# RWKV attention with a Sinkhorn-gated MoE on one core: the bonus term of the first six tiles, taken from the diagonal of the masked scores

## The chip, the cores and the metric

The kernel runs on one core of a Trainium2 chip. Its time is device microseconds (us) of one execution, and the time before is the median of three runs: 1522.19 us (1521.31 to 1522.67). One more execution was taken with the hardware profiler; every duration below is from that one. Its five instruction streams are PE (TensorE, matmuls and transposes), DVE (VectorE), ACT (ScalarE), POOL (GpSimd) and SP, which here only issues DMAs. Each works through its own instructions in a fixed order, and waits for the others by semaphores.

## The reference

Two parts follow each other. The first is a linear attention with a decaying state for each of 4 batches and 8 heads, 768 tokens and a head dimension of 48; the second is a mixture of 8 experts over the 3072 x 384 rows that come out, whose gate is balanced by eight Sinkhorn rounds.

```python
for t in range(S):
    kt, vt, rt = (k[:, :, t], v[:, :, t], r[:, :, t])
    cur = np.einsum('bhd,bhe->bhde', u[None] * kt, vt)
    y[:, :, t] = np.einsum('bhd,bhde->bhe', rt, state + cur)
    state = w[None, :, :, None] * state + np.einsum('bhd,bhe->bhde', kt, vt)
...
for e in range(E):
    h = np.maximum(x @ w1[e], 0.0)
    ye = h @ w2[e]
    out += P[:, e:e + 1] * ye
```

The term with `u` is the bonus: token t sees its own value with the weight sum over d of r·u·k, one number for each token and head. All other tokens that t sees come through the state.

## The kernel before

**Tiles and stages.** The 3072 tokens are 24 tiles of 128 (6 tiles for a batch, `NCHB`). One loop, `for i in range(NTT + 3)` at line 852, runs the attention of all tiles as a software pipeline, and puts the matmuls of expert 0 (`g1_unit`, `g2_half`, handed out by `work`) between the tiles' steps, from iteration 4 on. After it come fourteen half experts, which are matmuls nearly back to back. Iteration i of the loop writes, in this order:

- `prep(i+2)`: r and k of tile i+2 are multiplied by tables of powers of w (`rtab` on POOL into `rp`, `ktab` on DVE into `kp`).
- `scale_x(i-2)`, `stage_e(i-2)`: the finished rows of tile i-2 are scaled and split in two float16 parts (`xsc`: the high part on ACT, the low part on DVE), then transposed by a DMA. For tile 2 PE does that (`turn_x`).
- `bonus_dot(i+1)`: POOL computes r·k and then r·k·u (`rk`).
- `stage_b(i+1)`: PE transposes `rp` and `kp`, ACT copies the results out of PSUM (`rT`, `kT`).
- loads of r and k of tile i+4.
- `bonus(i)`: DVE sums `rk` over d (`dg`), POOL multiplies v by it and adds a tile of zeros or channels done apart (`xadd`, in `hbx`).
- `stage_c(i)`: PE makes the scores (`pA`), DVE writes those below the diagonal over a tile of zeros (`at`, by `copy_predicated` under a mask). Since the mask never touches the rest, the two tiles `at_[0]` and `at_[1]` are filled with zeros once.
- `state_part`, `scores_part` of tile i-1 (`py`: state and scores times v), `state_product(i)` (`pu`), then DVE's `sum_x(i-1)` (`x` = `py` + bonus), `state_sum(i)` (`S`; POOL scales it), and `bound_x(i-1)` (`xm`, `xs`: the row's scale).
- at the places "loads", "early", "masked", "middle" and "end" the steps of `hooks`: the split of expert 0's weights into float16 pairs, by `magnitude` (ACT), `column_sums` (PE, `pcs`), `scale` (DVE), `high` (ACT), `low` (DVE).

**What sets the order.** It is the order written out in the program: the wrapper `InOrder` keeps each engine's instructions as they come. SP's DMA queue is in program order as well. PSUM has four banks for the attention (`ps3`), taken in turn by `prT`, `pkT`, the two `pA` and the two `py`; so a transpose of the next tile waits until the scores that held its bank have been read.

**The opening.** `spin(n)` issues n matmuls on zeros (`pz`) which compute nothing that is used. Ahead of the loop the tables are built: w is clamped (`wsafe`), its powers are scanned, inverted and transposed (`pt_tab`, copied by ACT to `rtab` and `ktab`). In the same stretch `hbx` (9216 columns) is zeroed by three engines, and a flag is computed on DVE which says whether any w lies out of range. Every engine loads the flag and branches past `scan_channels`, a slow path which these inputs do not take.

Of the kernel before, what the change touches and what calls it, by code (L numbers as in the profile page):

```python
# [33 lines left out]
def rwkv_sinkhorn_moe(  # L34
# [364 lines left out]
    fill(at_[0].rearrange("p h c -> p (h c)"))  # L399
# [4 lines left out]
    wlim = part(hb3, F32, 2496, (H, D))[:1]  # L404
    flag = ac.tile([1, 1], F32, name="flag")
# [5 lines left out]
    def scan_channels(scratch):  # L411

        BH = B * H
        yd = scratch.tile([B, S, DM], F32, name="yd")
        rows = [part(hbx, F32, i * BH * D, (BH, D))[:D] for i in range(4)]
        kb, rb, stt, kv = rows
        wn, wbad, wz = (part(hbx, F32, 4 * BH * D + i * H * D, (H * D,))[:D] for i in range(3))
        vt, yv = (part(hbx, F32, 5 * BH * D + i * BH, (BH,))[:D] for i in range(2))
        G.dma_start(wn, w.rearrange("(o h) d -> o (h d)", o=1).broadcast_to([D, H * D]))
        V.tensor_scalar(wbad, wn, W_MAX, W_MIN, op0=ALU.min, op1=ALU.max)  # L420
        V.tensor_tensor(wbad, wn, wbad, op=ALU.not_equal)
        V.memset(wz, 0.0)
        V.copy_predicated(wz, wbad.bitcast(I32), wn)
        V.memset(stt, 0.0)

        def of_b(x_):
            return x_.rearrange("p (b h) d -> p b (h d)", b=B)

        def for_b(x_):
            return x_.unsqueeze(1).broadcast_to([D, B, H * D])  # L430

        with tc.For_i(0, S, 1) as t:
            for dst, src in ((kb, k), (rb, r)):
                G.dma_start(
                    dst,
                    src.rearrange("b h s d -> s (b h) d")[bass.ds(t, 1)].broadcast_to([D, BH, D]),
                )
            G.dma_start(vt, v.rearrange("b h s d -> s d (b h)")[bass.ds(t, 1)].rearrange("o d a -> (o d) a"))
            V.tensor_tensor(rb, rb, stt, op=ALU.mult)
            V.tensor_reduce(yv, rb, axis=AX.X, op=ALU.add)  # L440
            for b in range(B):
                G.dma_start(
                    yd[b].rearrange("s (h d) -> s d h", d=D)[bass.ds(t, 1)].rearrange("o d h -> (o d) h"),
                    yv[:, b * H : (b + 1) * H],
                )
            V.tensor_tensor(of_b(kb), of_b(kb), for_b(wbad), op=ALU.mult)
            V.tensor_tensor(kv, kb, vt.unsqueeze(2).broadcast_to([D, BH, D]), op=ALU.mult)
            V.tensor_tensor(of_b(stt), of_b(stt), for_b(wz), op=ALU.mult)
            V.tensor_tensor(stt, stt, kv, op=ALU.add)
        yt = yd.rearrange("b s d -> (b s) d").rearrange("(t p) d -> p t d", p=P)  # L450
        for t in range(NTT):
            G.dma_start(xadd(t), yt[:, t, :])

    bad = nc.values_load(flag.bitcast(I32), min_val=0, max_val=0x3F800000)
    with tc.If(bad > 0):
        with tc.tile_pool(name="scratch", bufs=1, space=bass.MemoryType.DRAM) as scratch:
            scan_channels(scratch)

    load_part(2, "v", v)
    load_part(3, "v", v)  # L460
# [329 lines left out]
    def work(n, ready=True, hold=False):  # L790
        if not ready:
            spin(3)
            return
# [588 lines left out]
```

## Time and profile before

| what | before |
|---|---|
| median of three runs | 1522.19 us |
| the profiled execution | 1522.51 us, of which the span from the first to the last instruction is 1521.0 us |
| granted TensorE clock, mean | 0.999 |
| instructions | 29000 |
| zero matmuls (`pz`) | 52, the last at 36.1 us |

The rest of the profile is shown in the prediction, beside what is read from it. Nearly all lines of the trace carry line 30, that of the wrapper, so instructions are told apart by the names of what they write and read. A timeline row gives start, duration, engine, line, operation, output, inputs, shape and number; what follows in brackets is the idle time of that engine ahead of the row and what ended it. "SPq" and "ACTq" are DMA issues. A row of the view of stretches gives start and end, length, busy time and number for PE, PEld (weight loads), DVE, ACT and POOL, then the granted TensorE clock, the DMA share and GB/s.

### The profile page before, as it was taken

What the parts mean: (1) busy time and instruction counts of PE and PEld (TensorE: products, weight loads), DVE (VectorE), ACT (ScalarE), POOL (GpSimd) and SP (SyncE); (2) the same over time, 40 slices, a digit from 0 to 9 for tenths busy, and PEclk for the clock granted to TensorE, in tenths of its full rate; (3) what the DMA queues carried; (4) which work ended last, traced back from release to release, by engine and by line L of the source; (5) the groups of instructions that cost most, each with busy time, mean ns of one, the idle gap of its engine ahead of it and who ended that gap; (6) DMA issues with size and microseconds to landing.
All of it is one profiled execution on the core that took longest, in us unless ns stands there. A gap on an engine that the chain in (4) does not pass through costs nothing.

```text
span 1521.0 us, 29000 instructions
## 1 busy us (share of the span) xinstructions
PE 1502.5 (99%) x11729; PEld 848.4 (56%) x11729; DVE 1015.7 (67%) x1692; ACT 672.8 (44%) x1203; POOL 588.0 (39%) x685
## 2 busy tenths in 40 slices
PE   8899999999999999999999999999999999999999
PEld 5677765555555555555555555555555555555555
DVE  8898869586566666666676666666566666566464
ACT  5444435344354544545454444444354444445320
POOL 8779966010214234242524234242424233242200
PEclk9999999999999999999999999999999999999999
DMA  9756523211344675666656675655554554555434
GB/s 176 155 113 125 106 60 103 87 37 58 103 84 73 92 130 86 118 89 122 95 77 124 92 130 83 120 63 96 61 84 68 61 98 57 100 57 98 58 94 130
DMA packets 186441, 143.10 MB, mean 94 GB/s; under 512 B 108737, under 2 KB 180162, under 8 KB 186306
## 3 DMA queue, kind: packets, MB, share of 16 engines
q0 software_dynamic: 44928, 61.36, 32.8%
q1 hardware_dynamic: 141168, 79.87, 20.3%
q8 instruction: 92, 1.51, 0.4%
q14 instruction: 43, 0.35, 0.1%
q10 hardware_dynamic: 210, 0.00, 0.0%
HBM read 55.39 MB, written 80.23 MB: 89 GB/s over the span
## 4 chain that ended last, share of the span: by engine, by line
PE 93%; DVE 3%; POOL 1%; issue 1%; ACT 0%; DMA 0%; SPq 0%; POOLq 0%; DVEq 0%; ACTq 0%
PE po L30 49%; PE bZ L30 12%; PE bY L30 12%; PE ph L30 5%; PE bA L30 5%; PE bB L30 5%; PE bC L30 2%; PE py L30 2%; PE pA L30 1%; POOL rk L30 1%; DVE at L30 0%; PE pkT L30 0%; PE prT L30 0%; DVE xsc L30 0%; PE px L30 0%
## 5 line engine op out<-in xcount | busy, mean ns | idle before, releaser
L30 PE MATMUL po<-ws,hbx 128*128 128x384 f16 x3360 | 736.8, 326 | 0.0
L30 POOL DMA_DIRECT2D accd<-stg x288 | 250.5, 870 | 694.4 <-ACT stg L30 679.5
L30 PEld LDWEIGHTS <-hbx 128*128 128x128 f16 x3504 | 333.4, 98 | 292.1
L30 PEld LDWEIGHTS <-ws 128*128 128x128 f16 x3096 | 301.6, 98 | 248.5 <-issue 4.7
L30 ACT ACTIVATE hbx<-tb 128x512 f16<-128x512 f32 x224 | 141.0, 630 | 453.0 <-DVE tb L30 453.0
L30 PE MATMUL po<-ws,hb 128*128 128x384 f16 x1248 | 322.8, 326 | 0.0
L30 DVE TENSOR_TENSOR tb<-bY,tb 128x512 f32<-128x512 f32 x168 | 116.2, 692 | 176.3 <-PE bY L30 176.1
L30 ACT ACTIVATE stg<-po,pe 128x384 f32<-128x384 f32 x312 | 179.1, 574 | 122.1 <-PE po L30 99.1
L30 PE MATMUL bZ<-xv,ws 128*128 128x512 f16 x840 | 227.0, 379 | 0.8 <-DVE tb L30 0.8
L30 PE MATMUL bY<-xv,ws 128*128 128x512 f16 x840 | 227.0, 379 | 0.0
L30 DVE TENSOR_TENSOR tb<-bZ,tb 128x512 f32<-128x512 f32 x168 | 115.5, 687 | 135.8 <-PE bZ L30 135.8
L30 PEld LDWEIGHTS <-hb 128*128 128x128 f16 x1248 | 121.5, 98 | 93.0
L30 POOL TENSOR_TENSOR ucb<-rawb 128x256 f32<-128x256 f32 x84 | 75.8, 952 | 118.8 <-DMA rawb<-in_moe_w_dram 118.8
L30 DVE TENSOR_TENSOR tb<-bB,tb 128x512 f32<-128x512 f32 x112 | 77.4, 691 | 49.3 <-PE bB L30 47.4
L30 PE MATMUL ph<-hbx,ws 128*128 128x384 f16 x576 | 104.1, 326 | 3.0 <-issue 1.8
L30 DVE SCALAR_TENSOR_TENSOR hb<-tb,hbx 128x512 f16<-128x512 f32 x112 | 77.2, 689 | 24.6 <-ACT hbx L30 19.5
L30 PE MATMUL bA<-xv,ws 128*128 128x512 f16 x336 | 90.8, 379 | 0.0
L30 PE MATMUL bB<-xv,ws 128*128 128x512 f16 x336 | 90.8, 379 | 0.0
L30 DVE SCALAR_TENSOR_TENSOR hbx<-tb,hbx 128x512 f16<-128x512 f32 x112 | 78.8, 704 | 14.7 <-ACT hbx L30 10.4
L30 ACT COPY tb<-bZ 128x512 f32<-128x512 f32 x56 | 32.8, 586 | 65.4 <-PE bZ L30 65.4
L30 DVE SCALAR_TENSOR_TENSOR hb<-ph,hb 128x384 f16<-128x384 f32 x64 | 34.9, 551 | 28.8 <-ACT hb L30 28.3
L30 ACT ACTIVATE hb<-ph 128x384 f16<-128x384 f32 x64 | 31.0, 490 | 48.7 <-PE ph L30 48.3
(165 smaller groups left out, 1500.7 us busy)
## 6 DMA issues: line engine op xcount, KB each, us to landing
accd<-stg POOLq DMA_DIRECT2D x288, 192.0 KB, 3.7
rawb<-in_moe_w_dram SPq DMA_DIRECT2D x28, 768.0 KB, 8.0
e0d<-stg SPq DMA_DIRECT2D x48, 192.0 KB, 2.0
hb<-e0d SPq DMA_DIRECT2D x48, 192.0 KB, 3.8
vn<-in_v_dram SPq DMA_DIRECT2D x24, 192.0 KB, 4.4
accd<-stg SPq DMA_DIRECT2D x24, 192.0 KB, 1.8
accd<-hb POOLq DMA_DIRECT2D x24, 192.0 KB, 4.7
rawb<-accd SPq DMA_DIRECT2D x24, 192.0 KB, 2.4
```

The source lines that it names most:

```text
L30: return lambda *a, **k: self.tc.keep_in_program_order(f(*a, **k))
```

## The change

For tiles 0 to 5 (`ND` = 6) the bonus no longer passes through POOL's four products and DVE's sum. POOL multiplies the transposed `rT` by `kT` (`diagonal_product`, 128x512), PE sums that over d with a 128x2 matrix of u·w for each pair of heads (`diagonal_sums`, `pd`, four matmuls of two columns), ACT copies the 8 sums of each token (`dgs`), and ACT then writes, for each head, the identity matrix scaled by these sums over the whole score tile (`diagonal`, 8 instructions of 128x128). DVE's masked copy then puts the scores below that diagonal. So v is weighted by both in one product, and `x` is `py` plus the zeros of `hbx`. Tile 0's sums are made from r·k·u on POOL and DVE, since it has no iteration ahead of it. From tile 6 on the bonus is as before, and ACT zeroes both score tiles again in iterations 6 and 7 (`reset_scores`).

`prep` moves `kp` from DVE to POOL for tiles 2 to 7. `stage_b(1)`, which stood in the middle of iteration 0, is put where it stands in the other iterations. The `spin` calls of iterations 0 to 3 go, and in the opening 15 + 4 zero matmuls stay of 19 + 5 + 4. The zeroing of `hbx` is cut in eight pieces over four places. The flag is computed on ACT by two Relu sums, and the branch comes after tile 0's diagonal. Loads are in another order: u comes third, r and k run one tile further ahead in the first iterations, and the second weight load of expert 0 comes in iteration 2 and no longer in 1; its `magnitude` moves from "early" to "last" of iteration 3. `scan_channels` gains the bonus of its channels for tokens from 128 on; it is not entered here. `wbd` is written by ACT, four instructions of 128x48.

```diff
+    cuts = [0, 2240, 2816, 3264, 4800, 6080, 6976, 8128, 9216]
+    zero = [hbx[:, a_:b_] for a_, b_ in zip(cuts, cuts[1:])]
...
-    fill(hbx[:, 2 * HB :])
-    spin(19)
+    fill(zero[5])
+    S_.activation(wlim, wflat, AF.Relu, bias=edge[:, 0:1], accum_out=sides[:, 0:1])
+    S_.activation(wlim, wflat, AF.Relu, bias=edge[:, 1:2], scale=-1.0, accum_out=sides[:, 1:2])
+    S_.activation(wlim[:, :2], sides, AF.Copy, accum_out=flag)
+    spin(15)
...
-    V.tensor_scalar(wlim, wrow, W_MAX, W_MIN, op0=ALU.min, op1=ALU.max)
-    V.tensor_tensor(wlim, wlim, wrow, op=ALU.not_equal)
-    V.tensor_reduce(flag, wlim, axis=AX.XY, op=ALU.max)
...
+    def diagonal(tt):
+        for h in range(H):
+            S_.activation(at_[tt % 2][:, h], ident, AF.Copy, scale=dgs[tt % 2][:, h : h + 1])
...
     def prep(tt):
         ld_ = loads[tt]
         G.tensor_tensor(rp_[tt % 2][:, :, :D], ld_["r"], rt4, op=ALU.mult)
-        V.tensor_tensor(kp_[tt % 3][:, :, :D], ld_["k"], kt4, op=ALU.mult)
+        (G if 2 <= tt <= ND + 1 else V).tensor_tensor(kp_[tt % 3][:, :, :D], ld_["k"], kt4, op=ALU.mult)
...
+    def diagonal_product(tt):
+        d = st[tt]
+        q = at2.tile([P, NPAIR, P], F32, tag="q", name=f"q_{tt}", bufs=1)
+        G.tensor_tensor(q, d["rT"], d["kT"], op=ALU.mult)
+        d["q"] = q
+
+    def diagonal_sums(tt):
+        q = st[tt].pop("q")
...
+        for p_ in range(NPAIR):
+            T.matmul(
+                pd[:, 2 * p_ : 2 * p_ + 2], q[:, p_], uw[:, p_], start=True, stop=True,
+                skip_group_check=True,
+            )
+        S_.copy(dgs[tt % 2], pd)
...
-    hook(1, "early", 0, "magnitude", 0)
-    hook(1, "loads", 0, "load", 1)
-    hook(2, "early", 0, "column_sums", 0)
+    hook(2, "early", 0, "magnitude", 0)
+    hook(2, "middle", 0, "column_sums", 0)
     hook(2, "middle", 0, "scale", 0)
+    hook(2, "loads", 0, "load", 1)
     hook(3, "early", 0, "high", 0, 0)
     hook(3, "early", 0, "high", 0, 1)
-    hook(3, "early", 0, "magnitude", 1)
     hook(3, "masked", 0, "low", 0, 0)
+    hook(3, "last", 0, "magnitude", 1)
     hook(3, "last", 0, "low", 0, 1)
...
+        if ND <= i + 1 < NTT:
+            bonus_dot(i + 1)
         if i + 1 < NTT:
-            bonus_dot(i + 1)
-        if i + 1 < NTT and i:
             stage_b(i + 1)
+        if i + 1 < ND:
+            diagonal_product(i + 1)
...
-        if i < NTT:
+        if i in (ND, ND + 1):
+            reset_scores(at_[i % 2])
+        if ND <= i < NTT:
             bonus(i)
+        if 1 <= i < ND:
+            diagonal(i)
...
-        if i < 4 or i > 10:
-            work(1, i > 4)
+        if i > 10:
+            work(1)
...
         if i < NTT:
             state_product(i)
+        if i + 1 < ND:
+            diagonal_sums(i + 1)
```

How the instructions then stand on the engines is shown at three places. The first is ACT in iterations 1 and 2 of the loop. Before, with `ws` the first magnitude, `xsc` the high part of tile 0 and then of tile 1, and `rT`, `kT` the copies for tiles 3 and 4:

```order
L30 ACTIVATE ws_75<-ws_74 128x1536
L30 ACTIVATE xsc_533<-x_514,xs_521 128x384
L30 COPY rT_545<-prT_540 128x512
L30 COPY kT_552<-pkT_547 128x512
L30 ACTIVATE xsc_680<-x_657,xs_664 128x384
L30 COPY rT_692<-prT_687 128x512
L30 COPY kT_699<-pkT_694 128x512
```

The same place now, from the sums of tile 2 (`dgs`) to the copies for tile 4:

```order
L30 COPY dgs_195<-py_1_502 128x8
L30 ACTIVATE xsc_569<-x_556,xs_563 128x384
L30 COPY rT_578<-prT_573 128x512
L30 COPY kT_585<-pkT_580 128x512
L30 ACTIVATE at_180<-ident,dgs_195 128x128 x8
L30 ACTIVATE ws_75<-ws_74 128x1536
L30 COPY dgs_196<-py_1_627 128x8
L30 ACTIVATE xsc_718<-x_697,xs_704 128x384
L30 COPY rT_727<-prT_722 128x512
L30 COPY kT_734<-pkT_729 128x512
```

The eight writes of a diagonal now stand behind `xsc`, `rT` and `kT` of their iteration. The second place is DVE in iteration 2, from the scale of tile 0 to the rows of tile 1. Before:

```order
L30 RECIPROCAL xs_521<-inv_s 128x1
L30 TENSOR_TENSOR kp_171<-kn_343,ktab 128x8x48
L30 SCALAR_TENSOR_TENSOR xsc_533<-x_514,xs_521,xsc_533 128x384
L30 TENSOR_REDUCE dg_559<-rk_413 128x8
L30 COPY_PREDICATED at_173<-mask,pA_0_571 128x4x128
L30 COPY_PREDICATED at_173<-mask,pA_1_572 128x4x128
L30 TENSOR_TENSOR x_657<-py_0_591,rk_338 128x4x48
L30 TENSOR_TENSOR x_657<-py_1_592,rk_338 128x4x48
```

And now:

```order
L30 RECIPROCAL xs_563<-inv_s 128x1
L30 SCALAR_TENSOR_TENSOR xsc_569<-x_556,xs_563,xsc_569 128x384
L30 COPY_PREDICATED at_180<-mask,pA_0_606 128x4x128
L30 COPY_PREDICATED at_180<-mask,pA_1_607 128x4x128
L30 TENSOR_TENSOR x_697<-py_0_626,hbx 128x4x48
L30 TENSOR_TENSOR x_697<-py_1_627,hbx 128x4x48
```

`kp` and `dg` are gone from between two tiles' masked copies, and the copy now writes a tile that ACT wrote last. The third place is ACT from iteration 3 to 4. Before, with `xsc` the high part of tile 2 and the copies for tile 5:

```order
L30 ACTIVATE ws_75<-ws_74,sw_0_111 128x768 x2
L30 ACTIVATE ws_75<-ws_74 128x1536
L30 ACTIVATE xsc_822<-x_803,xs_810 128x384
L30 COPY rT_834<-prT_829 128x512
L30 COPY kT_841<-pkT_836 128x512
```

And now:

```order
L30 ACTIVATE ws_75<-ws_74,sw_0_113 128x768 x2
L30 COPY dgs_195<-py_1_776 128x8
L30 ACTIVATE xsc_859<-x_846,xs_853 128x384
L30 ACTIVATE ws_75<-ws_74 128x1536
L30 COPY rT_869<-prT_864 128x512
L30 COPY kT_876<-pkT_871 128x512
L30 ACTIVATE at_180<-ident,dgs_195 128x128 x8
```

The second magnitude (the 128x1536 row) stood ahead of tile 2's `xsc`, and now stands between it and the copies for tile 5. PE's sums of it (`pcs`) stand in both kernels between the transposes for tile 5 and the scores of tile 4.

More of the change, by code (lines that the diff above doesn't have):

```diff
@@ L309, in rwkv_sinkhorn_moe, with load_uw @@
     S_.dma_start(wt[HP : HP + D, :], wr[1])
+    ND = NCHB
+    uw = ac.tile([P, NPAIR, 2], F32, name="uw")
+    V.memset(uw, 0.0)
+    def load_uw():
+        ur = u.rearrange("(p two) d -> two d p", two=2)
+        for g in range(2):
+            Q.dma_start(uw[g * HP : g * HP + D, :, g], ur[g])
     zeros = ac.tile([P, TB], F16, name="zeros")
@@ L366, in rwkv_sinkhorn_moe @@
     )
-    G.memset(hbx[:, :HB], 0.0)
+    cuts = [0, 2240, 2816, 3264, 4800, 6080, 6976, 8128, 9216]
+    zero = [hbx[:, a_:b_] for a_, b_ in zip(cuts, cuts[1:])]
+    G.memset(zero[0], 0.0)
+    edge = ac.tile([1, 2], F32, name="edge")
+    sides = ac.tile([1, 2], F32, name="sides")
+    flag = ac.tile([1, 1], F32, name="flag")
+    V.memset(edge[:, 0:1], -W_MAX)
+    V.memset(edge[:, 1:2], W_MIN)
     V.memset(unit, 0.0)
@@ L370, in rwkv_sinkhorn_moe @@
     V.memset(step[:, :, 0:1], 0.0)
-    V.memset(hbx[:, HB : 2 * HB], 0.0)
+    V.memset(zero[3], 0.0)
     def fill(x_):
@@ L398, in rwkv_sinkhorn_moe @@
         G.memset(t_[:, :, D:], 0.0)
[L399 removed]
+    G.memset(zero[1], 0.0)
     rk0 = at2.tile([P, H, D], F32, tag="rk", name="rk_0", bufs=3)
     G.tensor_tensor(rk0, loads[0]["r"], loads[0]["k"], op=ALU.mult)
[L404 to L408 removed]
@@ L411, in scan_channels @@
[L411 to L460, printed above, removed]
+    G.tensor_tensor(rk0, rk0, ub, op=ALU.mult)
+    G.memset(zero[2], 0.0)
+    dgs = [ac.tile([P, H], F32, name=f"dgs{i}") for i in range(2)]
+    def diagonal(tt):
+        for h in range(H):
+            S_.activation(at_[tt % 2][:, h], ident, AF.Copy, scale=dgs[tt % 2][:, h : h + 1])
@@ L494, in rwkv_sinkhorn_moe @@
+    bad = nc.values_load(flag.bitcast(I32), min_val=0, max_val=0x7F800000)
+    with tc.If(bad > 0):
+        with tc.tile_pool(name="scratch", bufs=1, space=bass.MemoryType.DRAM) as scratch:
+            scan_channels(scratch)
+    load_part(4, "r", r)
+    load_part(4, "k", k)
+    W[0]["load"](0)
+    load_part(2, "v", v)
+    load_part(5, "r", r)
+    load_part(5, "k", k)
+    load_part(3, "v", v)
     onesb = ac.tile([P, P], BF16, name="onesb")
@@ L788, in prepare, with work @@
             side.pop(0)()
[L790 to L793, printed above, removed]
+    def work(n, hold=False):
         held[0] = hold
@@ L848, in rwkv_sinkhorn_moe @@
     stage_b(0)
-    bonus_dot(0)
-    S_.copy(onesb, ones)
-    S_.copy(ident16, ident)
+    for p_ in range(NPAIR):
+        wc = pw[:, p_, HP : HP + 1]
+        S_.activation(wbd[:, p_], wc.broadcast_to([P, D]), AF.Copy, scale=wc)
+    V.tensor_tensor(uw, uw, wsafe.unsqueeze(2).broadcast_to([P, NPAIR, 2]), op=ALU.mult)
     for i in range(NTT + 3):
@@ L871, in rwkv_sinkhorn_moe @@
         run(i, "loads")
-        if i < NTT:
+        if i in (ND, ND + 1):
+            reset_scores(at_[i % 2])
+        if ND <= i < NTT:
             bonus(i)
+        if 1 <= i < ND:
+            diagonal(i)
+        if i == 1:
+            S_.copy(onesb, ones)
+            S_.copy(ident16, ident)
         leave(1)
         run(i, "early")
-        if i < 4 or i > 10:
-            work(1, i > 4)
+        if i > 10:
+            work(1)
         if i < NTT:
```

118 lines of the change are left out of this document (88 added, 30 removed).

## The prediction

> **What bounds the kernel now.** I read the page first (its shares by engine), then the view of stretches over the loop, then the timeline of the loop's first iterations.
>
> ```profile
> PE 1502.5 (99%) x11729; PEld 848.4 (56%) x11729; DVE 1015.7 (67%) x1692; ACT 672.8 (44%) x1203; POOL 588.0 (39%) x685
> 0.00:43.69 43.69, 35.91 (x794) 23.99 (x794) 36.13 (x71) 21.64 (x31) 36.88 (x45) 1.00 0.84 161
> 43.69:63.38 19.69, 17.28 (x361) 12.80 (x353) 18.45 (x42) 8.43 (x15) 16.81 (x17) 0.91 0.86 192
> 63.38:110.00 46.62, 45.38 (x1091) 33.55 (x1090) 42.30 (x86) 20.78 (x38) 31.12 (x33) 1.00 0.62 123
> 0.00:43.69 43.69, 14.88 (x52) 1.00 0.84 161
> 20.00:30.00 10.00, 10.00 (x320) 7.62 (x319) 8.36 (x20) 3.49 (x6) 9.69 (x11) 1.00 1.00 194
> ```
>
> PE is busy in 99% of the span, so its work after the opening is fixed and only the start can change. Up to 43.69 us, where the first matmul of expert 0 begins, PE idles 43.69 - 35.91 = 7.8 us and spends 14.9 us (the row with 52 `pz`) on zeros. From 43.69 to 63.38 it idles 2.4 us more, and to 110 another 1.2 us. So the question is when expert 0's matmuls start and how well they then run. POOL is busy 9.69 of 10 us in the early loop, and DVE hardly less. How they wait for each other is in the timeline from tile 1's masked copy to tile 2's:
>
> ```profile
> 21.57 1.40 DVE L30 COPY_PREDICATED at<-mask,pA 128x512 f32<-128x512 int32 x2 [1.51 <-PE pA L30]
> 22.86 0.61 DVE L30 TENSOR_TENSOR x<-py,rk 128x192 f32<-128x192 f32 x2
> 24.61 0.16 DVE L30 RECIPROCAL xs<-inv_s 128x1 f32<-128x1 f32 x1
> 24.69 0.92 DVE L30 TENSOR_TENSOR kp<-kn,ktab 128x384 f32<-128x384 f32 x1
> 24.80 0.62 ACT L30 ACTIVATE xsc<-x,xs 128x384 f16<-128x384 f32 x1 [2.88 <-DVE xs L30]
> 25.32 0.57 ACT L30 COPY rT<-prT 128x512 f32<-128x512 f32 x1
> 25.53 1.36 DVE L30 SCALAR_TENSOR_TENSOR xsc<-x,xs,xsc 128x384 f16<-128x384 f32 x1
> 25.79 0.59 ACT L30 COPY kT<-pkT 128x512 f32<-128x512 f32 x1
> 26.81 0.54 DVE L30 TENSOR_REDUCE dg<-rk 128x8 f32<-128x384 f32 x1
> 27.27 1.38 DVE L30 COPY_PREDICATED at<-mask,pA 128x512 f32<-128x512 int32 x2
> ```
>
> DVE works without a gap: copy, `x`, scale, `kp`, `xsc`, `dg`, next copy. The copy's end, W(i) for tile i, goes from 22.97 to 28.65, a period of 5.7 us. ACT does `xsc`, `rT`, `kT` beside it and then has nothing to do.
>
> **The change, part by part.** *What DVE saves.* `kp` (0.92) and `dg` (0.54) leave the stretch between two copies, some 1.5 us a tile, and POOL loses four products of about 1.06 us for `kp` and one of 512 columns. That alone would shorten the period to about 4.3 us.
>
> *What ACT gets.* Eight writes of 128x128 with a scale read from memory. The trace has no such row, but both terms:
>
> ```profile
> L30 ACT CAST onesb<-ones 128x128 bf16<-128x128 f32 x1 | 0.3, 311 | 0.0
> 31.94 1.77 ACT L30 ACTIVATE ws<-ws,sw 128x768 f16<-128x768 f32 x2
> L30 POOL TENSOR_TENSOR rk<-rn,kn 128x384 f32<-128x384 f32 x6 | 6.3, 1056 | 0.0
> 40.13 1.71 POOL L30 TENSOR_TENSOR rp<-rn,rtab 128x384 f32<-128x384 f32 x1
> 19.14 0.47 PEld L30 LDWEIGHTS pkT<-ident,kp 128*128 128x128 f32 x4
> ```
>
> A 128x128 copy with a fixed scale takes 0.31 and overlaps its neighbour by 0.1: at least 8 x 0.2 + 0.1 = 1.7 us. With a scale read from memory `xsc` takes 0.62 for 384 columns, and two `ws` of 768 take 1.77, so one is 0.94: 0.32/384 = 0.84 ns a column and 0.29 fixed. Then 128 columns take 0.40, and eight 8 x 0.3 + 0.1 = 2.5 us at most. I take 2.4, nearer to the rows with a scale from memory. `q` on POOL is 1.056 x 512/384 = 1.4 us (1.06 if length did not count, 2.3 by the slow `rp` row). `pd` has four weight loads as in the PEld row, 0.5 us, and hardly any columns; I bound it by twice that. A tile's eight transposes take two such rows, about 1.0. The four `wbd` writes of 48 columns are 4 x (0.29 + 0.04 - 0.1) + 0.1 = 1.0.
>
> *The new loop.* In ACT's order the diagonal of tile i stands behind `xsc` of tile i-2, which waits for the scale that DVE computes after copy i-1; and copy i must wait for the diagonal. So one tile costs: from the copy's end to `xsc` 24.80 - 22.97 = 1.83; `xsc`, `rT`, `kT` until 26.38, 1.58; the diagonal 2.4 less 0.1 overlap; the copy 1.4. Sum **7.1 us** against 5.7. With the low end for the diagonal, 1.7, it is 6.4, with the high end 7.2. DVE's low part of `xsc` now lies beside ACT's part; nothing hides the diagonal. Behind the waiting copy DVE has `x`, `S`, `xm` and `xs` in its queue, so the next tile's `xsc` and, behind it on ACT, the next copies wait as well; PE waits for the bank that the masked copy frees. The other new waits have slack in this loop: `q` can begin with `kT` (3.4 after the copy) and ends at 4.8, by then PE does `py`, `pd` follows at about 5.3 to 5.8, and ACT copies the sums at 6, a microsecond before the next `x` wants them. If `q` took 2.3 this slack would nearly be gone. POOL's two `prep` products, `q` and `S` are some 4.4 us, under the period.
>
> *The opening.*
>
> ```profile
> 1.58 0.40 ACTq L30 DMA_DIRECT2D wt<-in_w_dram  x1
> wt<-in_w_dram ACTq DMA_DIRECT2D x1, 0.8 KB, 1.9
> 2.47 2.62 DVE L30 MEMSET hbx<- 128x3072 f32 x1 [0.58 <-issue]
> 7.19 0.17 DVE L30 TENSOR_SCALAR wsafe<-wt 128x4 f32<-128x4 f32 x1 [0.75 <-DVE flag L30]
> 12.14 0.59 ACT L30 COPY ktab<-pt_tab 128x512 f32<-128x512 f32 x1
> 12.76 3.52 DVE L30 TENSOR_TENSOR kp<-kn,ktab 128x384 f32<-128x384 f32 x3 [1.55 <-ACT ktab L30]
> 15.19 1.10 PE L30 MATMUL pA<-rT,kT 64*64 64x128 f32 x32
> 16.90 1.36 DVE L30 COPY_PREDICATED at<-mask,pA 128x512 f32<-128x512 int32 x2
> ```
>
> DVE's memset halves (-1.3), and its flag and the wait for it, which fill the 2.1 us from 5.09 to 7.19, go; a few tiny memsets come: `wsafe` starts near 2.5 + 1.3 + 0.1 = 3.9, 3.3 us earlier, and w is there by then (1.58 + 1.9 = 3.5). `ktab` is then done at 12.73 - 3.3 = 9.4. But tile 0's diagonal now waits for DVE: two `kp` of 3.52/3 = 1.17 and a sum of 0.54, 12.3; the diagonal 14.7; and `rT`, `kT` stand behind it, 15.7; `pA` 16.8; W(0) = **18.2**, before 18.26. What the flag's move wins, the diagonal takes back. The branch is covered by ACT's queued writes; uncovered it costs up to the 0.75 of DVE's wait. For tile 1 nothing overlaps: `wbd` 1.0, `rT` and `kT` 1.0, `q` 1.4, `pd` 0.5, the transposes of tile 2 which PE has behind `pd` 1.0, the last copy 0.5, the diagonal 2.4, the masked copy 1.4. W(1) = 15.7 + 9.2 = 24.9, before 22.97. W(2) = 32.0 (28.65), W(3) = 39.1.
>
> *Iteration 4 and expert 0.*
>
> ```profile
> 33.61 1.48 ACT L30 ACTIVATE ws<-ws 128x1536 bf16<-128x1536 f32 x1
> 33.90 1.33 DVE L30 COPY_PREDICATED at<-mask,pA 128x512 f32<-128x512 int32 x2
> 35.14 1.02 DVE L30 SCALAR_TENSOR_TENSOR ws<-ws,sw,ws 128x768 f16<-128x768 f32 x1
> 41.37 1.37 DVE L30 COPY_PREDICATED at<-mask,pA 128x512 f32<-128x512 int32 x2
> 43.69 1.64 PE L30 MATMUL ph<-hbx,ws 128*128 128x384 f16 x9
> 54.83 0.85 ACT L30 ACTIVATE hb<-ph 128x384 f16<-128x384 f32 x2
> 56.21 0.32 PE L30 MATMUL py<-S,rT 64*64 64x48 f32 x4 [1.89 <-ACT rT L30]
> 57.00:58.00 1.00, 1.00 (x44) 0.91 (x40) 1.00 (x3) 1.00 (x1) 0.50 (x1) 0.50 0.72 157
> 61.43 2.11 PE L30 MATMUL po<-ws,hb 128*128 128x384 f16 x12
> ```
>
> W(3) was 35.23 and W(4) 42.74. Now the low split of `ws` adds 1.0 to the period, and the second magnitude, which lay beside DVE's work, stands in ACT's chain with 1.4: W(4) = 39.1 + 7.1 + 2.4 = 48.6. Expert 0's `ph` started 0.95 after W(4), so at **49.5**, 5.8 us late.
>
> *The queue of loads.* u is moved past the loads of tile 1, which arrive later by one load, about 1 us at the 194 GB/s of the quoted stretch; tile 1's `kp` is wanted only at 10.6, so nothing waits. The two small loads of u's columns are hidden there too. The first weight load is put behind the branch and r and k of tile 4; its magnitude comes an iteration later. The second is put behind the transposing DMA of tile 0, which waits for `xsc` near 28.5, and four more loads: I estimate its issue at about 33.
>
> ```profile
> ws<-in_moe_w_dram SPq DMA_DIRECT2D x4, 768.0 KB, 5.2
> 62.63 0.55 DVE L30 TENSOR_TENSOR kp<-kn,ktab 128x384 f32<-128x384 f32 x1
> ```
>
> Such a load took 5.2 us to land, so 38.2, and it is wanted at 42.5; if loads queued behind the transpose took that cover of 4.3 us, the chain would be later by what is missing. (The second row is of use below: `kp` on DVE in a quiet moment.)
>
> Iteration 5: `ph` to 51.2, transposes and the copy of `kT` 52.8, diagonal and masked copy: W(5) = 56.5. Iteration 6 has no diagonal: low split 1.0, scale 1.6, `xsc` 0.5, two `hb` 0.85, `rT` 0.6: `py` begins at 61.0. From there to the end of `po` PE took 7.3 us (56.21 to 63.54), of which some 3 us ran at a granted clock of 0.50; without that, 1.5 less. `po` ends at 66.8, **3.3 us later** than 63.54. Behind that point PE has almost no idle time to give back (1.2 us up to 110). So 1522.5 (the profiled execution, 0.3 above the median) + 3.3 = **1525.8 us**. The zeroing in iterations 6 and 7 (1024 columns, by 0.84 ns each about 1 us of ACT) lies beside PE's matmuls. The removed spins cost nothing by themselves, as PE waits there for ACT.
>
> **The rivals.**
> *B: the clock drops.* In iteration 4 PE's `pcs` waits for the second magnitude, from about 40 to 43.8, with no zeros to fill it. After 1.89 us of idle at 54.3 the row shows 0.50 for 3 us. One such stage costs 1.5 us, and the late `ph` passes it on: 1527.5 to 1529. [...]
> *C: faster.* If ACT's diagonals lie beside DVE's work, as where the eight take 1.0 us or less, the period is below 5.7 and W(4) comes ahead of 42.74. At the full saving, 2.3 of each period, W(1) is 22.6, W(4) 39.4 and `ph` starts at 40.3, 3.4 early; without the slow stage, 1.5 more: 1517.6. For it speaks that POOL and DVE are full now; against it the order, in which no work of DVE stands between `xs` and the copy but `xsc`.
> *D: a wash.* `kp` takes 0.55 where POOL is quiet (-1.2 in the opening), and a masked copy may start when its own half of the heads is written (-0.3 in each of five): 1523.1.
>
> **How the numbers follow.** A difference under 0.2%, 3 us, is what a measurement cannot tell from none. The forecast (1523.5 to 1528) has 0.45, of which 0.33 lies above 1525.2; B, with a late weight load, 0.17; D 0.18; C 0.20. So slower 0.33 + 0.17 = 0.50, the same 0.12 + 0.18 = 0.30, faster 0.20. The range 1518.5 to 1530 holds all of the first and of D, most of B and nearly half of C; the forecast alone would reach from 1523.5 to 1528.
>
> **What would show it.** Right: eight `at` rows in about 2.4 us on ACT between `kT` and the masked copy, DVE idle ahead of that copy with "ACT at" as its releaser, W(1) to W(3) some 7 us apart, `ph` near 49.5, PE idle ahead of `pcs`. Wrong: DVE gapless with a period under 5.7, or `ph` before 43.7; or a trace in which PE catches up after 66 us, which I rule out by its 1.2 us of idle time.

## The result and the profile after

| | before | after |
|---|---|---|
| median of four executions | 1522.43 us (1521.31 to 1523.53) | 1532.93 us (1532.27 to 1534.20) |
| ratio, 95% interval | | 1.0070 [1.0053, 1.0087] |
| the profiled execution, its span | 1522.51, 1521.0 | 1533.58, 1532.1 |
| granted TensorE clock, mean | 0.999 | 0.994 |

The change makes the kernel 0.7% slower, 10.5 us, where 3.3 were predicted. The engines' line of the changed kernel's page:

```profile
PE 1505.4 (98%) x11736; PEld 853.8 (56%) x11736; DVE 1004.5 (66%) x1681; ACT 688.9 (45%) x1268; POOL 571.1 (37%) x676
```

From its view of stretches the part up to expert 0's first matmul (53.10), up to the end of its first `po` (72.76), and up to 110; then the zero matmuls alone, with PE's busy time and number only:

```profile
0.00:53.10 53.10, 38.62 (x801) 29.40 (x802) 29.66 (x63) 34.16 (x85) 27.13 (x39) 0.87 0.77 155
53.10:72.76 19.66, 17.45 (x356) 12.78 (x356) 15.95 (x39) 11.76 (x24) 13.06 (x13) 0.91 0.58 123
72.76:110.00 37.24, 36.34 (x889) 26.90 (x887) 33.26 (x71) 17.76 (x31) 22.51 (x24) 1.00 0.57 118
0.00:53.10 53.10, 6.02 (x19) 0.87 0.77 155
```

PE's busy time grew by 2.9 us over the span, though 33 zero matmuls are gone. Ahead of expert 0, PE idles 53.10 - 38.62 = 14.5 us (7.8 before) and spends 6.0 us on zeros (14.9 before). New is the third column from the right, the granted clock: 0.87 over the opening, where it was 1.00. Narrow stretches show where:

```profile
15.00:18.40 3.40, 2.29 (x52) 1.97 (x56) 0.21 (x1) 2.91 (x9) 0.41 (x1) 0.50 0.93 184
18.40:25.30 6.90, 6.46 (x97) 5.62 (x92) 1.40 (x3) 2.95 (x9) 4.05 (x4) 0.50 1.00 227
45.80:49.20 3.40, 3.17 (x40) 2.20 (x43) 1.04 (x2) 3.40 (x11) 1.27 (x1) 0.51 0.97 226
66.20:69.60 3.40, 3.40 (x123) 2.78 (x116) 2.69 (x7) 1.98 (x2) 3.32 (x4) 0.50 0.82 162
```

There are 17 us at half clock, from 15.0 to 25.3, from 45.7 to 49.2 and from 66.2 to 69.6, where the kernel before had one stage of 3.4 us at 56.5. PE's timeline shows the waits ahead of the stages and the longer durations in them:

```profile
16.11 1.98 PE L30 MATMUL pA<-rT,kT 64*64 64x128 f32 x32 [3.17 <-ACT kT L30]
19.32 1.87 PE L30 MATMUL pd<-uw,q 128*128 128x2 f32 x8 [0.44 <-POOL q L30]
26.18 1.05 PE L30 MATMUL py<-uw,q 128*128 128x2 f32 x8
46.03 1.44 PE L30 MATMUL pcs<-ws,onesb 128*128 128x384 bf16 x4 [4.09 <-ACT ws L30]
47.40 1.94 PE L30 MATMUL pA<-rT,kT 64*64 64x128 f32 x32
53.10 1.62 PE L30 MATMUL ph<-hbx,ws 128*128 128x384 f16 x9
65.41 0.32 PE L30 MATMUL py<-S,rT 64*64 64x48 f32 x4 [1.82 <-ACT rT L30]
66.68 1.51 PE L30 MATMUL py<-vn,at 128*32 128x48 f32 x64
119.84 1.64 PE L30 MATMUL ph<-hbx,ws 128*128 128x384 f16 x9 [1.62 <-DVE x L30]
```

`pA` takes 1.98 us instead of the 1.10 of before, and a tile's diagonal sums (`pd`; from tile 2 on they share a bank with `py`) take 1.87 at half clock and 1.05 at full, with 8 records for 4 matmuls. The loop itself, on DVE and ACT, between tile 1's masked copy and tile 2's:

```profile
25.76 1.36 DVE L30 COPY_PREDICATED at<-mask,pA 128x512 f32<-128x512 int32 x2 [5.97 <-ACT at L30]
28.95 0.16 DVE L30 RECIPROCAL xs<-inv_s 128x1 f32<-128x1 f32 x1
29.15 0.61 ACT L30 ACTIVATE xsc<-x,xs 128x384 f16<-128x384 f32 x1 [1.72 <-DVE xs L30]
30.14 0.59 ACT L30 COPY kT<-pkT 128x512 f32<-128x512 f32 x1
30.61 2.45 ACT L30 ACTIVATE at<-ident,dgs 128x128 f32<-128x128 f32 x8
32.81 1.36 DVE L30 COPY_PREDICATED at<-mask,pA 128x512 f32<-128x512 int32 x2 [1.73 <-ACT at L30]
```

The DVE that worked without a gap now waits for "ACT at" ahead of the copy, 13.0 us in five waits up to 110 us: four are for diagonals (11.0 us), the fifth, 1.97 us, is for the zeros of `reset_scores`. The period, copy end to copy end, is 34.17 - 27.12 = 7.05 us.

### The profile page after: what moved, and what is told of

Read it like the earlier page. It is cut to its first block, busy times and chain, and to the rows that moved or that the text cites. A ratio compares the mean times of both kernels' runs of the same rounds, so it can differ in the third digit from the quotient of the medians.

```text
span 1532.1 us, 29065 instructions
## 1 busy us (share of the span) xinstructions
PE 1505.4 (98%) x11736; PEld 853.8 (56%) x11736; DVE 1004.5 (66%) x1681; ACT 688.9 (45%) x1268; POOL 571.1 (37%) x676
## 3 DMA queue, kind: packets, MB, share of 16 engines
q0 software_dynamic: 44928, 61.36, 31.2%
## 4 chain that ended last, share of the span: by engine, by line
PE 91%; DVE 2%; issue 1%; ACT 0%; DMA 0%; SPq 0%; DVEq 0%
PE po L30 48%; PE bZ L30 12%; PE bY L30 12%; PE ph L30 5%; PE bA L30 5%; PE bB L30 5%; PE bC L30 2%; PE py L30 1%; PE pA L30 1%; PE pkT L30 0%; PE prT L30 0%; PE px L30 0%; DVE tb L30 0%; DVE wms L30 0%; DMA rn<-in_r_dram 0%
## 5 line engine op out<-in xcount | busy, mean ns | idle before, releaser
L30 DVE SCALAR_TENSOR_TENSOR hb<-ph,hb 128x384 f16<-128x384 f32 x64 | 35.0, 551 | 30.7 <-ACT hb L30 30.4
```

What stands on the lines that cost most here:

```text
L30: return lambda *a, **k: self.tc.keep_in_program_order(f(*a, **k))
```

## The experiments

All times are medians of the device time; the kernel before, on the same chips, had medians of 1521.95 to 1522.15. The changed kernel's 1532.93 stands beside 1522.43, so a difference to it carries up to 0.5 us of that; the ratios don't. "From" names the kernel that was edited; "Z" stands for zero matmuls in PE's waits, "M" for the late magnitude. The last column is the time at half clock in the profiled execution, up to 105 us.

| run | from | edit | us (range) | ratio to before, 95% | half clock |
|---|---|---|---|---|---|
| e1 | after | Z | 1528.80 (1528.34 to 1529.26) | 1.0046 [1.0030, 1.0063] | 3.4 |
| e2 | after | one write per diagonal | 1529.62 (1527.40 to 1531.23) | 1.0047 [1.0031, 1.0064] | 20.5 |
| e3 | after | M | 1530.13 (1527.31 to 1530.95) | 1.0049 [1.0033, 1.0066] | 20.5 |
| e4 | after | diagonal for tile 0 alone | 1529.89 (1529.66 to 1531.95) | 1.0058 [1.0042, 1.0075] | 10.2 |
| e5 | after | Z, M | 1527.86 (1525.57 to 1529.46) | 1.0034 [1.0021, 1.0046] | 3.4 |
| e6 | e5 | one write | 1526.44 (1523.65 to 1529.02) | 1.0027 [1.0015, 1.0038] | 6.8 |
| e7 | e5 | diagonal for tile 0 alone | 1521.69 (1521.31 to 1522.99) | 0.9997 [0.9987, 1.0007] | 0 |
| e8 | before | zeros in iteration 6 | 1522.11 (1521.10 to 1523.41) | 0.9999 [0.9990, 1.0009] | 3.4 |
| e9 | before | 33 zeros gone | 1524.31 (1522.32 to 1525.81) | 1.0014 [1.0004, 1.0023] | 10.2 |
| e10 | e6 | one matmul for the sums | 1518.92 (1517.96 to 1520.12) | 0.9976 [0.9967, 0.9986] | 0 |
| e11 | e5 | one matmul for the sums | 1522.87 (1522.23 to 1523.11) | 1.0005 [0.9995, 1.0014] | 0 |
| e12 | e5 | every write twice | 1544.33 (1542.84 to 1544.56) | 1.0148 [1.0131, 1.0165] | 17.1 |
| e13 | e5 | writes earlier | 1528.22 (1525.89 to 1529.66) | 1.0039 [1.0025, 1.0053] | 3.4 |
| e14 | e5 | sums in bf16 | 1522.93 (1521.88 to 1524.55) | 1.0006 [0.9997, 1.0016] | 0 |
| e15 | e13 | sums in bf16 | 1519.97 (1518.80 to 1522.87) | 0.9986 [0.9976, 0.9995] | 0 |
| e16 | after | sums in bf16 | 1529.25 (1528.77 to 1529.64) | 1.0046 [1.0029, 1.0063] | 13.7 |
| e17 | e15 | its zeros gone | 1522.61 (1520.83 to 1524.86) | 1.0004 [0.9995, 1.0014] | 13.7 |

### The zeros (e1, e9, e8)

e1 puts 62 zero matmuls where the changed kernel's PE waits. (In e5 and the runs made from it the 18 are left out, and iterations 4 and 5 get 3 ahead of `stage_c` too.)

```diff
+        if i == 0:
+            spin(16)
...
+        if i == TH + 1:
+            spin(18)
         run(i, "early")
...
+        if i in (1, 2, 3):
+            spin(3)
         if i < NTT:
             stage_c(i)
+        if i == 6:
+            spin(7)
...
+        if i == 0:
+            spin(3)
         if i + 1 < ND:
             diagonal_sums(i + 1)
+        if i in (1, 2, 3):
+            spin(3)
```

> The changed kernel with zero matmuls put back wherever its trace shows PE waiting in iterations 0 to 4 and 6 (16 + 3 in iteration 0, 3 + 3 in iterations 1 to 3, 18 ahead of the second column sums in iteration 4, 7 in iteration 6); nothing else differs. Theory K (the clock is a second, separate cost): the stages at 0.50 (15.0 to 25.3, 45.7 to 49.2, 66.1 to 69.6) go, the first masked copy ends near 18.3 and the second near 24.9 (19.56 and 27.12 now), the period stays at 7.05, and the time falls from 1532.9 by 2.2 + 1 + 1.5, to about 1528. Theory L (the loop through ACT's diagonals is all of the loss): PE waits there anyway, the time changes by less than 1 us. Rival S (the removed zeros are all of the loss): the period falls below 6 and the time comes back to 1523 to 1524.

e9 takes from the kernel before those zeros that the change removes, and nothing else:

```diff
-    spin(19)
+    spin(15)
...
-    spin(5)
...
         if not ready:
-            spin(3)
             return
...
-            if i == TH:
-                spin(3)
```

> The kernel before without the zero matmuls that the change removes, and nothing else: 4 of the opening's 19, the 5 ahead of the table transposes, and 3 at two places in each of iterations 0 to 3; 33 in all. K (the zeros hold the clock in PE's waits, and that is what their removal costs): one or more half-clock stages of 3.4 us between 10 and 45 us, 6 to 14 us at half clock where the kernel before has 3.4, and 1524 to 1527. P (the sum of the prediction: the removed zeros cost nothing, as PE waits there for ACT or DVE): within 0.5 us of the kernel before.

The view of stretches, first of e1, then of e9:

```profile
10.00:20.00 10.00, 8.75 (x106) 5.45 (x106) 5.14 (x7) 5.25 (x16) 5.71 (x6) 1.00 0.92 193
20.00:30.00 10.00, 9.79 (x281) 7.72 (x285) 4.33 (x10) 6.95 (x22) 5.99 (x7) 1.00 0.78 157
```

```profile
10.00:20.00 10.00, 8.22 (x104) 6.28 (x108) 7.55 (x14) 4.59 (x10) 7.46 (x7) 0.83 0.99 225
40.00:50.00 10.00, 8.41 (x168) 6.02 (x163) 7.52 (x17) 3.29 (x7) 9.25 (x10) 0.66 0.56 139
```

In e1 the clock is 1.00 from 10 to 30 us (one stage is left, from 32.7 to 36.1), and the kernel is 4.1 us faster than the changed one, though it does 62 matmuls more: they lie in waits. Of the 62, 25 stand in iterations 4 and 6, where the kernel before has none, so 4.1 us is not the price of the 33 removed zeros alone. e9 prices just these, in the kernel before: nothing else is missing, the stages come (0.83 and 0.66; one in the opening came once with all zeros in place too, in e8 below), and the time rises by 2.2 us, in K's range and out of P's. So both from the side of after and from that of before, the zeros have a price when they go. What the zeros do here is hold the clock: the time at half clock goes from 17.1 us to 3.4 when e1 adds zeros to the changed kernel, and from 3.4 to 10.2 when e9 takes them from the kernel before.

e8 asks if the same helps the kernel before, ahead of its one stage:

```diff
         if i < NTT:
             stage_c(i)
+        if i == 6:
+            spin(7)
```

> The kernel before with 7 zero matmuls behind the scores of iteration 6, where PE waits 1.89 us for ACT ahead of its only half-clock stage (56.5 to 60.2). K (that wait brings the half clock, and the half clock costs time where PE is the bound): the stage is gone and the time is 1.2 to 1.9 us under the kernel before, 1520.3. Z (the zeros delay as much as the clock gains, or the stage comes at the next wait): within 0.5 us of the kernel before.

Two stretches of e8, then a wait of PE in e8 and the longest near it in the kernel before:

```profile
10.00:20.00 10.00, 8.99 (x105) 6.68 (x106) 7.86 (x14) 4.34 (x10) 7.61 (x7) 0.83 0.89 205
50.00:60.00 10.00, 9.44 (x199) 6.39 (x198) 9.86 (x19) 3.72 (x6) 8.28 (x8) 1.00 0.89 186
```

```profile
75.26 0.24 PE L30 MATMUL py<-vn,kp 128*32 128x48 f32 x2 [1.74 <-issue]
```

```profile
76.45 2.44 PE L30 MATMUL ph<-hbx,ws 128*128 128x384 f16 x14 [0.92 <-issue]
```

The stage at 56.5 is gone (1.00), but in the profiled execution there is one in the opening (0.83), and the time is the same: Z. In that execution the first `po` ends 1.3 us earlier (62.26 against 63.54), which is lost again by the masked copy of tile 9 (83.61 against 82.95). In between PE stands still for 1.74 us with no wait that the profile shows, against 0.92 in the kernel before; that is 0.8 of it. The rest, and whether the other executions lose it in the same way, isn't settled.

### The second magnitude's place (e3, e5)

```diff
-    hook(3, "last", 0, "magnitude", 1)
-    hook(4, "early", 0, "column_sums", 1)
+    hook(4, "early", 0, "magnitude", 1)
+    hook(4, "middle", 0, "column_sums", 1)
```

> The changed kernel with the second magnitude moved behind the diagonal of iteration 4 and its column sums from early to middle of that iteration. Theory M (the magnitude in ACT's chain is a term of its own, 1.4 us, and its 4.1 us of PE waiting drops the clock): the masked copies of tiles 3 and 4 come 8.1 apart instead of 9.6, the stage at 0.50 from 45.7 goes, expert 0 starts at 50 to 51 instead of 53.1, and the time falls by 2 to 3 us to about 1530.4. If the iteration is bound elsewhere (PE's own work behind it): less than 0.7 us.

> The changed kernel with zero matmuls laid into PE's waits (16 and 3 in iteration 0, 3 and 3 in iterations 1 to 3, 3 in iterations 4 and 5, 7 in iteration 6) and the second magnitude and its column sums moved into iteration 4, behind that iteration's other work. A (clock and place of the magnitude are separate costs): the zeros alone gave 1528.8, the place alone 2.8 less than the changed kernel, so 1526.0 (1525 to 1527), with one half-clock stage of 3.4 us or none, and W(3) to W(4) near 7 us where the zeros alone had 9.2. N (both fill the same wait ahead of the column sums): 1528.8, no gain over the zeros alone. D (the place is worth more once the clock holds): 1524 or less.

e3 has W(3) to W(4) at 7.9 us for 9.6 and is 2.8 us faster than the changed kernel, as theory M had it. But the half clock didn't go as M had it: there is more of it, one stage from 48.3 on, and expert 0 starts at 52.5, not at 50 to 51. On top of the zeros (e5 against e1) the medians differ by 0.9 with overlapping ranges, and the zeros differ too, so whether the place costs something beside the clock isn't shown.

### The writes on ACT, and what else the change brought (e2, e4, e6, e7, e12)

e2 and e6 write a tile's diagonal in one instruction:

```diff
-        for h in range(H):
-            S_.activation(at_[tt % 2][:, h], ident, AF.Copy, scale=dgs[tt % 2][:, h : h + 1])
+        S_.activation(
+            at_[tt % 2], ident.unsqueeze(1).broadcast_to([P, H, P]), AF.Copy, scale=dgs[tt % 2][:, 0:1]
+        )
```

e4 and e7 leave the diagonal to tile 0 alone, and `kp` on DVE:

```diff
-    ND = NCHB
+    ND = 1
...
-        (G if 2 <= tt <= ND + 1 else V).tensor_tensor(kp_
+        V.tensor_tensor(kp_
```

e12 issues each write of tiles 1 to 5 twice:

```diff
-        for h in range(H):
+        for h in [h for h in range(H) for _ in range(2 if tt else 1)]:
```

> The changed kernel, in which each diagonal is one write of 128x1024 with one scale in place of eight of 128x128 (all heads get the sum of the first one, so the output is not the reference's). By the rows such a write takes 0.29 + 1024 x 0.84 ns = 1.15 us instead of 2.45. Theory L (the eight writes stand in a loop of DVE and ACT): the period between masked copies of tiles 1, 2, 3 falls from 7.05 to 5.75, each of the six diagonals gives 1.3 us, expert 0 starts near 46 and the time falls to about 1526. Rival S (clock and zeros) or the queue of loads: the period stays at 7, the time within 1 us of 1532.9.

> The changed kernel with the diagonal for tile 0 alone: from tile 1 on the bonus goes over POOL and DVE as before, with kp on DVE, and the opening, the loads and the missing zeros stay as in the change. Theory L: the period of tiles 1 to 3 is that of before, 5.7 to 6.6, the masked copy of tile 4 ends near 44.5 to 45.5 (50.81 now, 42.74 before), and the time falls by 5 to 7 us to about 1527; what is left over 1522.4 is the opening and the clock. Rival O (the opening and the order of loads are the cost, the diagonals are beside it): the time stays above 1530.

> As e5, and the eight diagonal writes of a tile become one write of 128x1024 with the scale of one head, so the bonus of the other heads is left wrong in its values but not in its amount of work. The write took 1.15 us in the earlier run against 2.45. L (ACT's eight writes set the loop of five iterations): the period falls from 6.9 to 5.7-6.4, 0.6 to 1.2 us in each of five iterations, 3 to 6 us in all: 1520 to 1523 if e5 gives 1526. P (the loop would be bound by PE's or DVE's own work anyway): within 1 us of e5.

> As e5, with the diagonal for tile 0 alone; the bonus of the other tiles is computed on GpSimd as in the kernel before. S (loop, clock and place of the magnitude are the whole loss; the opening and the order of the loads cost nothing): 1521 to 1523, as the kernel before. O (opening or loads have a price of their own): 1525 or more, with the second weights awaited by ACT ahead of the magnitude in iteration 4 (1.2 us with the diagonal for tile 0 alone and no zeros).

> The run with zeros and late magnitude (1527.9) with each diagonal write of tiles 1 to 5 issued twice, the same values to the same place: 8 more writes, 2.45 us more on ACT in each of five iterations. L (ACT's writes are on the loop, copy to copy): the period of iterations 2 and 3 grows from 7.0 to 9.4 and the time by 10 to 12.3, to 1538 to 1540. I (ACT has slack there and another engine sets the period): 1533 or less.

e12 settles that the writes are on the loop. ACT and DVE in its timeline, then the same copy in e5:

```profile
42.55 5.93 ACT L30 ACTIVATE at<-ident,dgs 128x128 f32<-128x128 f32 x16
47.78 1.47 DVE L30 COPY_PREDICATED at<-mask,pA 128x512 f32<-128x512 int32 x2 [4.76 <-ACT at L30]
```

```profile
37.95 1.37 DVE L30 COPY_PREDICATED at<-mask,pA 128x512 f32<-128x512 int32 x2 [1.71 <-ACT at L30]
```

Sixteen writes take 5.93 us, 3.5 more than eight (the expectation had 2.45), and five iterations of 3.5 would be 17.4; the time rose by 16.5. The copy waits 4.76 us for ACT, where it waits 1.71 in e5. e12 also has 13.7 us more at half clock, but the period grows without it: W(2) to W(3), at full clock up to 47.7, takes 10.55 us (38.70 to 49.25) for 7.07.

Taking the writes away showed less than expected: e2 gave 3.3 us, with 20.5 us at half clock, and e6 1.4 us under e5. e4 had the short periods of before in W(1) to W(3), but then 11.5 us to W(4):

```profile
40.58 1.48 ACT L30 ACTIVATE ws<-ws 128x1536 bf16<-128x1536 f32 x1 [1.16 <-DMA ws<-in_moe_w_dram]
42.11 1.44 PE L30 MATMUL pcs<-ws,onesb 128*128 128x384 bf16 x4 [6.05 <-ACT ws L30]
```

There PE waits 6.05 us for the second magnitude, and ACT for its weights. With zeros and the late magnitude the same edit gives e7, equal to the kernel before. So the new opening, the order of the loads and the flag's move cost nothing that can be measured here (S); the loss lies in the diagonals, the missing zeros and the magnitude's place (the last by the clock or beside it). e6 fell short of 1520 to 1523, and is out of P's range too. Up to W(5) its periods are 4.6 to 8.2 us but for W(2) to W(3) with 10.8, and most of that one is at half clock. PE's timeline of e6 there, and the stretch:

```profile
31.19 0.28 PE L30 MATMUL py<-vn,kp 128*32 128x48 f32 x3 [1.48 <-issue]
32.85 1.44 PE L30 MATMUL pz<-zeros 128*128 128x512 f16 x3
```

```profile
31.60:38.40 6.80, 6.80 (x25) 4.14 (x24) 3.48 (x12) 2.39 (x5) 2.80 (x4) 0.51 0.89 204
```

What the writes are worth is plainest between e11 and e10 of the next section, which have no half clock: one write for eight gives 3.95 us there (1522.87 to 1518.92).

### The sums on TensorE (e10, e11, e14, e16)

e10 and e11 sum with one matmul for four:

```diff
-        for p_ in range(NPAIR):
-            T.matmul(
-                pd[:, 2 * p_ : 2 * p_ + 2], q[:, p_], uw[:, p_], start=True, stop=True,
+        T.matmul(
+            pd, q[:, 0], uw.rearrange("p a two -> p (a two)"), start=True, stop=True,
```

In e14 and e16 `q` is bf16, and so is `uwb`, which takes the product that went to `uw`:

```diff
-        q = at2.tile([P, NPAIR, P], F32, tag="q", name=f"q_{tt}", bufs=1)
+        q = at2.tile([P, NPAIR, P], BF16, tag="q", name=f"q_{tt}", bufs=1)
...
-                pd[:, 2 * p_ : 2 * p_ + 2], q[:, p_], uw[:, p_], start=True, stop=True,
+                pd[:, 2 * p_ : 2 * p_ + 2], q[:, p_], uwb[:, p_], start=True, stop=True,
...
-    V.tensor_tensor(uw, uw, wsafe.unsqueeze(2).broadcast_to([P, NPAIR, 2]), op=ALU.mult)
+    uwb = ac.tile([P, NPAIR, 2], BF16, name="uwb")
+    V.tensor_tensor(uwb, uw, wsafe.unsqueeze(2).broadcast_to([P, NPAIR, 2]), op=ALU.mult)
```

> The run with zeros and late magnitude (1527.9) with the eight writes kept, and the four diagonal sums of a tile as one matmul, so the bonus is left wrong in its values. T (the sums stand on the path from one masked copy to the next): 2 records instead of 8, 0.75 us less in each of five iterations: 1524 to 1525. H (hidden, as PE waits for ACT's writes there in any case): 1527 to 1528.

> The run with zeros, late magnitude and one write per tile (1526.4), and the four diagonal sums of a tile on TensorE become one matmul with all eight columns, so the bonus is left wrong in its values. L+pd (the eight writes and the sums on TensorE are all that the diagonals cost): 1522 to 1523, as with the diagonal for tile 0 alone. G (GpSimd's q and kp, or ACT's copies of the sums, cost too): 1524.5 or more.

> As the run with zeros and late magnitude (1527.9), with the products q and the weights of the diagonal sums in bf16, so that the four matmuls of a tile are 4 records of a narrower type and not 8; the sums carry bf16's rounding. R (the sums' time on PE is what the single matmul saved): 1522.5 to 1525, most of the 5.0 us that one matmul for four gave. W (what the single matmul saved was the work itself, four weight loads against one, not the type): 1526 to 1528.

> The changed kernel with bf16 products and weights in the diagonal sums, nothing else; the sums carry bf16's rounding. A (the sums cost by their time on PE, whatever the clock does): 4 to 5 us less than the changed kernel, 1528 to 1529. K (what the shorter sums saved with the zeros in place was a half-clock stage; without zeros other waits bring the stages all the same): 1530.5 or more, with 10 us or more at half clock.

Neither theory of e11 was right: the period of the loop stayed (6.84 and 7.07 us, as in e5), as H had it, and yet 5.0 us went. e10 lies below both of its theories, 7.5 us under e6 and under the kernel before, with 6.8 us of half clock gone. e14 did as e11 with all the work kept, as R had it. Where it goes is seen in iteration 4, where expert 0 begins and PE becomes the bound; PE in e5, then in e14:

```profile
46.03 1.05 PE L30 MATMUL py<-uw,q 128*128 128x2 f32 x8
48.99 1.18 PE L30 MATMUL pcs<-ws,onesb 128*128 128x384 bf16 x4 [1.90 <-ACT dgs L30]
49.96 2.99 PE L30 MATMUL ph<-hbx,ws 128*128 128x384 f16 x9
```

```profile
45.04 0.25 PE L30 MATMUL py<-uwb,q 128*128 128x2 bf16 x4
46.78 0.81 PE L30 MATMUL pcs<-ws,onesb 128*128 128x384 bf16 x4 [1.49 <-ACT hbx L30]
47.42 1.63 PE L30 MATMUL ph<-hbx,ws 128*128 128x384 f16 x9
```

From the start of the sums to the end of `ph` e5 takes 52.95 - 46.03 = 6.92 us and e14 49.05 - 45.04 = 4.01: 0.8 from the sums, 0.4 from the wait, the rest because `pcs` and `ph` run at half clock in e5. All ten executions of e11 had a mean clock of 0.999 or 1.000; the one of e5 with 1.000 took 1525.84, so, as far as one execution tells, 3 of the 5.0 us are the sums themselves and 2 the clock. e16, without zeros, gives 3.7 us, just under A's 4 to 5, with 13.7 us at half clock left of 17.1, so part of it may be the clock here too.

### A shorter version (e13, e15, e17)

```diff
-        if 1 <= i < ND:
-            diagonal(i)
...
         if i + 1 < ND:
             diagonal_sums(i + 1)
+            diagonal(i + 1)
```

> As the run with zeros and late magnitude (1527.9), all eight writes kept, but each tile's writes issued on ACT right behind the copy of its sums, one iteration earlier than in the changed kernel, where ACT waited 1.7 us for DVE's xs; values as in the reference. Place (the writes cost because they stand between kT and the masked copy): the period of iterations 2 and 3 falls from 7.0 to 6.0 or less and the time to 1523 to 1525. Length (ACT's total work per iteration sets the period): within 1 us of 1527.9.

> Both of the above together, all sums and writes kept, sums in bf16. If place and sums are the two remaining costs and each gives what the cut-down runs showed (one write and one matmul: 1518.9), 1518 to 1521, under the kernel before. If ACT's total work sets the loop: 1522.5 to 1525.

> The run with early writes, bf16 sums and late magnitude (1520.0) without its zero matmuls. K (the zeros carry the clock, here as in the other two kernels, where they were worth 2.2 and 4.1 us): 1522 to 1524.5, with 6 us or more at half clock. P (with the shorter loop PE's waits are too short for the clock to fall): within 0.7 us of 1520.0.

In e13 the place brought nothing: the period is 7.2 us (24.57 to 31.81). The masked copies of tiles 2 to 5 no longer wait for ACT, as Place would have it, but behind the copy of the sums the writes stand ahead of `xsc`, `rT` and `kT`, which PE needs for the next sums, so that by the order they are on a loop again, through PE. With sums of 0.25 us this loop is shorter. ACT in e13, then in e15:

```profile
26.90 2.45 ACT L30 ACTIVATE at<-ident,dgs 128x128 f32<-128x128 f32 x8
33.94 2.44 ACT L30 ACTIVATE at<-ident,dgs 128x128 f32<-128x128 f32 x8
```

```profile
31.11 2.45 ACT L30 ACTIVATE at<-ident,dgs 128x128 f32<-128x128 f32 x8
34.43 0.58 ACT L30 COPY kT<-pkT 128x512 f32<-128x512 f32 x1
37.14 0.17 ACT L30 COPY dgs<-py 128x8 f32<-128x8 f32 x1 [0.47 <-PE py L30]
37.34 2.45 ACT L30 ACTIVATE at<-ident,dgs 128x128 f32<-128x128 f32 x8
```

From write to write it is 33.94 - 26.90 = 7.04 us in e13 and 37.34 - 31.11 = 6.23 in e15; the 0.8 us between them is what the sums became shorter. e15 is faster than both kernels: 2.2 us under the kernel before, 13.0 under the changed one. It keeps the diagonals of six tiles, and rounds their sums to bf16. e17 takes its zeros away and loses 2.6 us.

## Why the prediction was too low

The table sets the prediction's steps beside the profiled execution; W(i) is the end of tile i's masked copy.

| step | predicted | measured | too early by |
|---|---|---|---|
| W(0) | 18.2 | 19.56 | 1.4 |
| W(1) | 24.9 | 27.12 | 2.2 |
| W(2), W(3) | 32.0, 39.1 | 34.17, 41.22 | 2.2, 2.1 |
| W(4) | 48.6 | 50.81 | 2.2 |
| `ph` | 49.5 | 53.10 | 3.6 |
| W(5) | 56.5 | 60.55 | 4.0 |
| `py` of iteration 6 | 61.0 | 65.41 | 4.4 |
| end of `po` | 66.8 | 72.76 | 6.0 |
| time | 1525.8 | 1533.58 | 7.8 |

**The new loop** was right. Eight writes took 2.45 us for 2.4, the period was 7.05 for 7.1, and iteration 4 took 9.59 for 9.5. That the period fits so closely is partly luck: `xsc` began 2.03 us behind the copy (27.12 to 29.15) for 1.83, and the copy began 0.25 us before the last write ended (32.81 and 33.06), as D had it, so that it added 1.11 us for 1.4. From W(1) to W(4) the error doesn't grow; e12 shows the mechanism by its dose.

**"The removed spins cost nothing by themselves, as PE waits there for ACT"** is the step that failed. That PE waits there is true, and it is why they cost when they go: here the clock falls in the wait (0.50 from 15.0 us, with PE waiting until 16.11) and slows the work behind it. In the opening PE waits 3.17 us for tile 0's `kT`, 10.2 us run at half clock, and this is most of the 2.2 us in W(1): with the zeros back (e1) W(1) is 25.36, 1.8 earlier. With 62 zeros in PE's waits (e1) the changed kernel is 4.1 us faster; the 33 removed ones by themselves were worth 2.2 us in the kernel before (e9), and in the changed one weren't measured alone. Rival B had the mechanism, but only for iteration 4 and for one stage of 1.5 us; that stage came too (45.7 to 49.2), and with the opening's 2.2 us B would have come to 1531.2 at most.

**`pd`, 0.5 us, "I bound it by twice that"**, was mis-sized: 1.05 at full clock, just past that bound, and 1.87 at half, 8 records where four were assumed. The prediction gave it slack beside ACT, and in the loop it has that (e11's period), but in the opening and from iteration 4 on it stands on PE's path: e16 got 3.7 us by making it 0.25, part of it perhaps by the clock.

**Iteration 4:** `ph` started 2.3 us after W(4), not 0.95. Of the 1.3 us more, about 1.0 are the tile's sums, which stand ahead of `ph` and which the 0.95 of the kernel before doesn't hold; the rest is that PE, out of its 4.09 us wait at half clock, came later to `pxT`. The **second weight load** was issued at 36.5, not 33. ACT doesn't wait for it: the magnitude began at 44.51, and with e4's 5.5 us to landing the load would be there near 42.0, so some 2.5 of the cover of 4.3 were left. In e4, where ACT came to it earlier, it waited 1.16 us.

**"Without that, 1.5 less"** failed as well: the half-clock stage of iteration 6 didn't go away, since its wait is there as before (1.82 us for `rT`, 1.89 in the kernel before). It makes 1.6 of the error.

**Behind `po`** 1.8 us came on top, of which 1.62 is one wait of PE for DVE's `x` at 118 us. e1 doesn't have that wait; what brings it isn't settled.

By the runs, each on the changed kernel alone, the zeros were worth 4.1 us, the late magnitude 2.8 and shorter sums 3.7; that is 10.6 together, and all three at once (e14) gave 10.0 and the time of the kernel before. That the sum fits is partly luck: zeros and magnitude together gave 5.1 (e5), not 6.9, and the sums 4.9 on top of them, not 3.7, as all three bear on the same half-clock stages. By the medians the diagonals with their loop are a cost of 1.2 us beyond that (e14 against e7, which has them for tile 0 alone), and with the shorter loop of e15 a gain of 1.7; in both cases the intervals of the ratios overlap.

## What to carry to other kernels

Matmuls that compute nothing may be there for the clock, as the 33 here were (2.2 us when they go, e9): before they are removed, look whether the wait they fill stays, and price what runs behind it at half clock. Price a matmul of two columns by its weight loads: here eight loads took 0.97 us of the 1.05, and in float32 there were two for each matmul. Where a helper engine works in order, look at what stands behind an instruction before you move it to an earlier place: in e13 `rT` and `kT`, which PE needs, stood behind the writes, and the move brought nothing (1528.22 us for 1527.86).
